# Idle fillers on the tensor engine: fewer, as small products on zeros

## The chip, the cores and the metric

The kernel runs on one core of one Trainium2 chip. The core has five engines with instruction streams of their own: the tensor engine (PE; its loads of the stationary operand are shown as PEld), VectorE (DVE), ScalarE (ACT), GpSimd (POOL) and SyncE (SP), which issues most transfers. The metric is the device time of one execution in microseconds (us), lower is better; the median of several executions is given.

## What is computed

Two stages follow each other. The first is a linear attention with decay, over 4 batches of 8 heads, 768 positions and a head size of 64, computed in blocks. The second multiplies its output, seen as 3072 rows of 512, by `w_in` (512 x 2048), applies a leaky ReLU, and multiplies by `w_out` (2048 x 512). The weights arrive as 64-bit floats and the rest as 32-bit floats.

```python
for b in range(nb):                       # blocks along the sequence
    intra = einsum('bhic,bhjc->bhij', qb, kb) * Dmask
    intra = einsum('bhij,bhjd->bhid', intra, vb)
    inter = einsum('bhid,bhde->bhie', qb * lam_pow, kv_state)
    out[:, :, sl] = intra + inter
    kv_state = lam_block * kv_state + einsum('bhsd,bhse->bhde', kb * rev_pow, vb)
x = out.transpose(0, 2, 1, 3).reshape(B * S, H * D)
h = x @ w_in
g = maximum(0.01 * h, h)
return g @ w_out
```

## The kernel before

The 3072 rows are cut into 24 chunks of 128 positions (index `c`), and four chunks make a group of 512 rows. For each chunk PE transposes k and q (L331), multiplies scores and key-value products in 64 x 64 quadrants into the PSUM tile `psc` and the outputs into `po` (both through `quad`, L286). VectorE multiplies the scores by the decay factors (L375) and adds the state (L380, L382). GpSimd scales k (L345), scaled q (L349) and the state (L385). ScalarE copies the transposes out of PSUM (L340, L341). A tiny copy out of `po` (L414) separates two groups of products that write the same bank.

The output of a chunk is split into three parts `xh`, `xl`, `xm` (L430, L431, L433)[...]. `w_in` is loaded as 64-bit words into three buffers `raw` (L485, issued from ScalarE's queue), put together as 32-bit floats (L497 to L504) and split into `wh`, `wl`, `wm` (L510 to L521). The first layer multiplies these parts (L561), one group of 512 rows and 256 of the 2048 columns at a time; its result goes to DRAM. The second layer reads it back and multiplies by the parts of `w_out` (L620). Loads of k and q (L311, two transfers each) and v (L316) are issued from SP.

The order in which each engine gets its instructions is made by the class `Plan` (L37). Every piece of work is registered with `add`, with an estimated duration and the names of what it reads and writes; `emit` (L81) simulates the engines and sorts the pieces. A second pass in `emit` (from L144) goes through the sorted list with delays that are a little more optimistic, and issues the real instructions. In this pass, the variable `soon` holds when each engine is expected to be free. Where PE is expected to stand idle between `soon["PE"]` and the next piece's time `t`, `plan.idle` is called, which is the function `busy` (L250). It issues transposes of the identity matrix into the bank `b1[0]`, a bank that isn't in use yet: the fillers. Their time isn't added to `soon`. The fillers end for good with the first piece that writes that bank (`plan.spare`, "b10"), a product of the first layer.

Before the planned work, `busy(WARM)` issues 9 fillers (L255). The identity that they read is written by GpSimd, by `make_identity` (L248). `plan.warm` (L258) is where the second pass takes PE to be free for the first time. The tile `raw[-1]` is the third of the buffers for `w_in`; its first load is the third of these loads.

## Time and profile before

| what | before |
|---|---|
| median of 3 runs | 626.7 us (626.27 to 627.1) |
| profiled execution, time | 626.15 us |
| profiled execution, span from first to last instruction | 623.6 us |
| PE busy | 613.9 us, 98% |
| VectorE / ScalarE / GpSimd busy | 297.9 / 281.2 / 91.7 us |
| DMA, mean over the span | 163 GB/s, 101.51 MB |
| fillers (L253) | 38, from 1.36 to 29.66 us |
| first product of the first layer (L561) | 29.46 us |

The page of the profile cuts the span into 40 slices of 15.6 us. PE busy is counted from instructions whose ends are modelled, and weight loads lie beside products on a line of their own. The chain that ended last follows from the last instruction back to what released each step. In a timeline, a line gives the start, the duration, the engine, the line of the code and the operation of a run of like instructions; in square brackets stands how long the engine idled before it and what ended that.

The 38 fillers are the 9 at the start and 29 in eleven idle stretches that the plan expected. In order these hold 2 (at 5.05 us), 6 (6.33), 1 (9.80), 1 (14.40), 1 (15.47), 1 (16.21), 4 (20.64), 2 (22.02), 3 (25.20), 1 (27.94) and 7 (28.68) fillers.

### The profile page before, as it was taken

The page shows a single profiled execution, that of the slowest core. Times are in us where ns is not written, and L with a number is a line of the kernel's source. Part 1 is how long each engine was busy: PE and PEld are TensorE (multiplying, and loading weights), DVE is VectorE, ACT ScalarE, POOL GpSimd, SP SyncE. Part 2 cuts the span into 40 slices and gives each one's busy share as a digit, 9 for nine tenths or more (in the row PEclk, how much of TensorE's full clock was granted, in tenths as well). Part 3 has the DMA queues.
Part 4 walks back from the last instruction along what each step waited for, and adds up shares of the span by engine and source line. Part 5 has one row for each costly group of instructions (what it writes and reads, how often), then busy time and mean ns, then how long its engine had stood idle before and what let it go on. Part 6 is the DMA issues. An engine that isn't in the chain of part 4 may idle for free.

```text
span 623.6 us, 13157 instructions
## 1 busy us (share of the span) xinstructions
PE 613.9 (98%) x5578; PEld 513.5 (82%) x5578; DVE 297.9 (48%) x366; ACT 281.2 (45%) x461; POOL 91.7 (15%) x95
## 2 busy tenths in 40 slices
PE   8899999999999999999999999999999999999997
PEld 7688888898888888888788888888888888888885
DVE  4799882400344333333145763735545454535531
ACT  3688875443577766664444722312222222314111
POOL 4852513300332222222000000000000000000000
PEclk9999999999999999999999999999999999999999
DMA  9998844632787778842455762432524333333201
GB/s 201 250 259 259 243 156 136 155 111 91 206 248 253 245 238 259 247 163 87 169 202 189 247 203 72 153 117 82 188 67 135 136 106 131 128 109 118 85 0 67
DMA packets 103706, 101.51 MB, mean 163 GB/s; under 512 B 78560, under 2 KB 80608, under 8 KB 103648
## 3 DMA queue, kind: packets, MB, share of 16 engines
q1 hardware_dynamic: 99152, 92.29, 47.3%
q10 hardware_dynamic: 4496, 8.39, 4.3%
q8 instruction: 43, 0.70, 0.5%
q14 instruction: 15, 0.12, 0.1%
HBM read 65.02 MB, written 35.65 MB: 161 GB/s over the span
## 4 chain that ended last, share of the span: by engine, by line
PE 96%; DMA 2%; SPq 0%; POOL 0%; DVE 0%; ACT 0%; issue 0%; DVEq 0%
PE b L561 43%; PE b L620 17%; PE po L620 11%; PE psc L620 10%; PE po L286 4%; PE pt L620 3%; PE psc L286 3%; PE po L331 2%; PE pt L331 2%; DMA att<-in_q_dram 2%; PE b L253 1%; DMA att<-in_k_dram 1%; SPq L311 0%; PE b L331 0%; POOL att L345 0%
## 5 line engine op out<-in xcount | busy, mean ns | idle before, releaser
L602 ACT ACTIVATE xh<-att 128x1024 fp32r<-128x1024 f32 x48 | 50.9, 1061 | 147.3 <-PE po L620 141.3
L603 DVE SCALAR_TENSOR_TENSOR xl<-att,xh 128x1024 fp32r<-128x1024 f32 x48 | 58.7, 1223 | 99.4 <-ACT xh L602 99.4
L561 PE MATMUL b<-xh,wh 128*128 128x512 f32 (+3 forms) x416 | 105.5, 377 | 0.0
L561 PE MATMUL b<-xl,wl 128*128 128x512 f32 (+3 forms) x416 | 105.4, 376 | 0.0
L561 PE MATMUL b<-xm,wm 128*128 128x512 f32 (+3 forms) x416 | 104.9, 381 | 0.0
L561 PEld LDWEIGHTS b<-xl,wl 128*128 128x128 f32 x416 | 75.5, 188 | 14.7 <-DVE wl L515 0.2
L561 PEld LDWEIGHTS b<-xh,wh 128*128 128x128 f32 x416 | 75.3, 188 | 14.3
L561 PEld LDWEIGHTS b<-xm,wm 128*128 128x128 f32 x416 | 73.5, 188 | 13.2
L579 ACT ACTIVATE b<-b 128x512 f32<-128x512 f32 (+2 forms) x98 | 56.7, 579 | 57.1 <-PE b L561 56.3
L582 ACT ACTIVATE gs<-b 128x512 f32<-128x512 f32 (+2 forms) x98 | 57.8, 590 | 48.7 <-PE b L561 40.2
L375 DVE TENSOR_TENSOR att<-psc,att 128x512 f32<-128x512 f32 x24 | 16.5, 688 | 128.3 <-PE psc L286 128.2
L620 PE MATMUL b<-wl,xl 128*128 128x512 f32 x192 | 74.7, 389 | 0.0
L620 PE MATMUL b<-wh,xh 128*128 128x512 f32 x192 | 74.7, 389 | 0.0
L605 DVE SCALAR_TENSOR_TENSOR xm<-xl,xh 128x1024 fp32r<-128x1024 f32 x48 | 58.8, 1226 | 4.8
L345 POOL TENSOR_TENSOR att<-att 128x512 f32<-128x512 f32 (+1 forms) x24 | 27.6, 1149 | 141.1 <-PE po L331 133.5
L620 PEld LDWEIGHTS b<-wh,xh 128*128 128x128 f32 x192 | 36.1, 188 | 7.5
L620 PEld LDWEIGHTS b<-wl,xl 128*128 128x128 f32 x192 | 36.0, 188 | 7.5
L385 POOL TENSOR_TENSOR att<-att 128x256 f32<-128x256 f32 x40 | 35.6, 889 | 28.7 <-DVE att L382 23.4
L620 PE MATMUL po<-wm,xm 128*128 128x512 f32 (+1 forms) x100 | 37.2, 381 | 0.7 <-ACT raw L642 0.7
L620 PE MATMUL psc<-wh,xh 128*128 128x512 f32 x96 | 37.4, 389 | 0.0
L620 PE MATMUL po<-wl,xl 128*128 128x512 f32 x96 | 37.4, 389 | 0.0
L620 PE MATMUL b<-wm,xm 128*128 128x512 f32 x96 | 37.4, 389 | 0.0
(67 smaller groups left out, 817.1 us busy)
## 6 DMA issues: line engine op xcount, KB each, us to landing
att<-g SPq DMA_DIRECT2D x48, 512.0 KB, 3.2
g<-gs SPq DMA_DIRECT2D x45, 512.0 KB, 2.9
raw<-in_moe_w_in_dram ACTq DMA_DIRECT2D x16, 512.0 KB, 5.0
raw<-in_moe_w_out_dram SPq DMA_DIRECT2D x16, 512.0 KB, 4.3
att<-in_k_dram SPq DMA_DIRECT2D x48, 128.0 KB, 4.0
att<-in_q_dram SPq DMA_DIRECT2D x48, 128.0 KB, 3.7
att<-in_v_dram SPq DMA_DIRECT2D x24, 256.0 KB, 3.9
out_dram<-gs SPq DMA_DIRECT2D x23, 256.0 KB, 2.2
```

The lines of the kernel that those rows point to most:

```text
L286: nc.tensor.matmul(dst[HALF[cols]], lhsT=lhsT[HALF[rows]], rhs=rhs[HALF[rows]], start=start, stop=True, skip_group_check=True)
L331: nc.tensor.transpose(out=at[y], in_=src[:, 2 * y:2 * y + 2, :].rearrange("p a d -> p (a d)"), identity=ident)
L345: lambda e="POOL": ENG[e].tensor_tensor(kr[nr], kr[nr], _bc(pow_k, 3, D)[nr], op=ALU.mult), ["fk"], [f"k{i}"])
L375: add("DVE", 0.69, lambda: nc.vector.tensor_tensor(sc, psc[:, :, lower, :], decay, op=ALU.mult), ["psc", "fk"], ["sc"])
L385: add("POOL", 0.7, lambda new=new, j=j: nc.gpsimd.tensor_tensor(state[(j + 1) % 4], new, _bc(lam_c, 2, D), op=ALU.mult), [f"st{j % 4}", "f ...
L561: nc.tensor.matmul(dst, lhsT=w[z][:, kk * 2 * P + f * P:kk * 2 * P + (f + 1) * P], rhs=x[z][:, kk, toks], start=start and kk == 0, stop=kk ...
L579: add("ACT", ns, lambda b=b: nc.scalar.activation(out=b, in_=b, func=AF.Copy, bias=0.0, scale=S + 1.0), [], [kb], rank=-1.5)
L582: add("ACT", ns, lambda b=b, r=r: nc.scalar.activation(out=r, in_=b, func=AF.Prelu, bias=0.0, scale=1.0 / WS, alpha=0.01), [kb], [f"gs{jg} ...
L602: add("ACT", 1.05, lambda: nc.scalar.activation(out=h, in_=graw[j], func=AF.Copy, bias=0.0, scale=NEAR), reads, wr("h"))
L603: add("DVE", 1.25, lambda: nc.vector.scalar_tensor_tensor(l, graw[j], 1.0, h.bitcast(F32), op0=ALU.mult, op1=ALU.subtract), reads + [f"rh{ ...
L605: add("DVE", 1.25, lambda: nc.vector.scalar_tensor_tensor(m, l.bitcast(F32), -S, h.bitcast(F32), op0=ALU.mult, op1=ALU.add), [f"rh{j}", f" ...
L620: nc.tensor.matmul(acc[tb][z // 2][:, cols], lhsT=ring[j][z][:, f * T + tb * P:f * T + (tb + 1) * P], rhs=W[pp][z][:, f * d_model:(f + 1) ...
```

## The change

Four things change. The second pass calls for fillers only where the expected idle time is over 1.0 us, not 0.4; and it asks for as many as fit into it less 0.8 us, not less 0.2, at 0.22 us each as before. A filler becomes a product of a 128 x 128 stationary operand with 64 columns, in place of a transpose of 128 columns. The number at the start goes from 9 to 12, and these read a 128 x 128 piece of `raw[-1]` that VectorE fills with zeros, not the identity from GpSimd; the later ones still read the identity. Last, `plan.warm` starts from 0.6 us instead of 1.3: with 12 for 9 fillers it goes from 3.28 to 3.24.

```diff
@@ -150,8 +150,8 @@
             if e == "PE":
                 if self.spare in self.ops[i][4]:
                     self.idle = None
-                if self.idle is not None and t > soon[e] + 0.4:
-                    self.idle(int((t - soon[e] - 0.2) / 0.22))
+                if self.idle is not None and t > soon[e] + 1.0:
+                    self.idle(int((t - soon[e] - 0.8) / 0.22))
             soon[e] = t + ways[e]
@@ -182,7 +182,7 @@
-    WARM = 9
+    WARM = 12
@@ -247,15 +247,17 @@
     nc.scalar.dma_start(out=lam_b, in_=lam.partition_broadcast(P))
     make_identity(nc, ident)
 
-    def busy(n):
+    def busy(n, x=ident):
 
         for _ in range(n):
-            nc.tensor.transpose(out=b1[0][:, 0:P], in_=ident, identity=ident)
-
-    busy(WARM)
+            nc.tensor.matmul(b1[0][:, 0:C2], lhsT=x, rhs=x[:, 0:C2], start=True, stop=True, skip_group_check=True)
+
+    idle = raw[-1][:, 0:P]
+    nc.vector.memset(idle, 0.0)
+    busy(WARM, idle)
     nc.gpsimd.memset(zero, 0.0)
     plan = Plan()
-    plan.idle, plan.spare, plan.warm = busy, "b10", 1.3 + 0.22 * WARM
+    plan.idle, plan.spare, plan.warm = busy, "b10", 0.6 + 0.22 * WARM
```

## The prediction

> **What bounds the kernel now.** I read the page first, then PE's waits, then the chain that ended last over the first 31 us, then the timeline there. From the page:

> ```profile
> PE   8899999999999999999999999999999999999997
> PEclk9999999999999999999999999999999999999999
> DMA  9998844632787778842455762432524333333201
> ```

> Each digit is 15.6 us. PE is full from the third slice on; only slices 0 and 1 leave room, and there DMA is the full one. All waits of PE in the run:

> ```profile
> PE pt L331 <- DMA att<-in_q_dram: 1.5, 2, 0.8
> PE b L253 <- POOL att L256: 1.4, 1, 1.4
> PE psc L286 <- DVE att L382: 1.0, 2, 0.7
> PE po L620 <- ACT raw L642: 0.7, 1, 0.7
> PE po L286 <- ACT att L414: 0.6, 2, 0.3
> PE b L331 <- DMA att<-in_k_dram: 0.5, 1, 0.5
> ```

> That is 5.7 us, and apart from 0.7 at 619 us and 0.3 at 307 us all of it lies before the first product of the first layer (L561). From there PE runs without a break, so only an earlier or later start of L561, at 29.66 us in the chain, can reach the end. The chain up to it (start, length, what):

> ```profile
> 4.01 1.25 PE b L331 x4
> 5.26 0.43 PE b L253 x2
> 5.69 0.85 PE pt L331 x4
> 6.54 1.28 PE b L253 x6
> 7.82 1.55 PE psc L286 x64
> ...
> 12.19 1.21 PE psc L286 x64
> ...
> 15.38 4.93 DMA att<-in_q_dram
> ...
> 20.80 0.44 PE b L253 x4
> 21.24 0.82 PE po L286 x45
> 22.05 4.61 DMA att<-in_q_dram
> ...
> 28.75 0.91 PE b L253 x7
> ```

> The fillers (L253) stand on the chain five times: before q0's transposes, before the first scores, at 20.80, at 28.01 (0.26, not shown) and for 0.91 us right before L561. The two loads of q, 4.93 and 4.61 us from issue to landing against a median of 3.7, lie between.

> [...]four transposes take 0.85 us at 5.69 and 0.44 later, so 0.213 and 0.11 each. [...]between 1.36 and 7.8 PE did nothing but transposes, fillers among them, at half clock; the first products start at 7.75, and within their 1.55 us the distance of four concurrent ones goes from 0.107 to 0.058, at 8.8 us. PEclk doesn't show this change. [...]Here q5's second half, issued at 22.05, lands at 26.66, beside a load of w_in issued from ACT at 22.17.

> **The change part by part.** The sum is made against the profiled execution, 626.15 us with a span of 623.6; the median of three is 626.7, so 0.55 is added at the end.

> *Which fillers are left.* The planned gaps don't change, since fillers don't enter the plan's times. Before, a gap got int((gap-0.2)/0.22) fillers; after, int((gap-0.8)/0.22), and none up to 1.0. From the counts of the timeline (2, 6, 1, 1, 1, 1, 4, 2, 3, 1, 7: 29): the gap of 6 was 1.52 to 1.74 us and gets 3 or 4; that of 4 was 1.08 to 1.30 and gets 1 or 2; that of 3 gets 0 or 1; that of 7 was 1.74 to 1.96 and gets 4 or 5; all others none. So 8 to 12 are left of 29.

> *What one costs.* It loads 128 columns of weights and moves 64, where a transpose moves 128. Weight loads that nothing holds up:

> ```profile
> 4.01 0.29 PEld L331 LDWEIGHTS b<-att 128*128 128x128 f32 x2 [0.87 <-DMA att<-in_k_dram]
> 22.02 0.20 PEld L253 LDWEIGHTS b<-att 128*128 128x128 f32 x2
> ```

> One load alone is 0.18 (slow clock) or 0.14; the second adds 0.11 or 0.06. The 64 columns take 0.107 or 0.058, as the scores show. So a filler takes 0.11 (slow) or 0.06 (full) where load and product overlap, and 0.21 or 0.12 where they don't. I take the lower, since here loads of different products do overlap, and keep both. So a filler covers half of what the transpose did at most, and the plan's 0.22 twice too much.

> *The warm-up.* VectorE's fill is off the trace; its nearest row is GpSimd's fill of the same size, 0.20 us from 0.73. VectorE has nothing to do until 3.43, so nothing queues behind it. PE starts at about 1.0 instead of 1.36, and 12 fillers end between 2.3 (12 x 0.11) and 3.5 (12 x 0.21). The first half of k lands at 3.96 either way: cost nothing, gain nothing. Only the clock could gain. The loads into the third buffer of raw (whose zeros the fillers read) come third in order, at 22.17: no wait there.

> *The first scores.* Without the two fillers at 5.26, q0's transposes are held by q0's landing (5.07 and 5.64) and by their own 0.85: they end at 6.12 instead of 6.54. Then 3 or 4 fillers, 0.33 to 0.84, end by 6.96. Keys and values for psc are there at 6.60 (GpSimd's L345, 5.54 + 1.06) and 6.87 (v's landing). So psc starts at about 6.95 instead of 7.82: PE is 0.85 earlier, 0.3 more if the clock rises earlier. k1's second half lands at 8.05, so its transposes can follow at once, and psc of chunk 1 comes at about 11.3 instead of 12.19.

> *What becomes of that lead.* Behind psc stand the loads of k3 and q3 on SP. But the DMA engines are full: landings follow each other about 0.57 us apart from 4 to 12 us, and the view by windows of one us has their share at 0.96 to 1.37 from 7 to 16 us (packets of several queues are summed) and 0.81 in the next. SP's issues themselves take 1.5 us there instead of 0.5. An earlier issue only fills what was free: 0.2 of the us at 16. q3 then lands between 0 and 0.6 us earlier; I take 0.2, the free time, and 0.6 for the range.

> *The gaps at 20.8 and later.* The four fillers at 20.80 hold po 0.44 us; with one or two short ones po comes 0.3 earlier. That gains nothing: what follows waits for ACT's copy (L414, 22.58), behind three other ACT operations that start with q3's transposes, and then for DVE's L382, until 24.11. The two at 22.02, three at 25.20 and one at 27.94 end before their next operation is released anyway (ACT 22.80, q5 26.71, ACT 28.29).

> *The last gap.* L561 needs xh of chunk 3:

> ```profile
> 28.81 0.60 ACT L430 ACTIVATE xh<-po 128x512 fp32r<-128x512 f32 x1
> ```

> It is there at 29.41; the seven fillers end at 29.66. Four or five short ones end at 28.75 + 0.6 = 29.35 at most. L561 starts at about 29.46: 0.20 gained, the one sure gain. Next late is ACT's xh.

> *After it.* PE is full, but three weight loads of wl (46.88, 56.32, 77.22) waited for DVE's L515 by 0.23, 0.08 and 0.07: DVE's splitting of w_in has no slack there. Part of that work follows PE, since ACT waits for PE's products before it (at 41.27, for one); part hangs on w_in's loads. Either 0.2 + 0.2 = 0.4 us comes through whole, or the wl at 46.88 holds PE and next to nothing does. I take 0.4, because ACT's waits say that the work ahead of this wl moves with PE, and keep 0 for the range.

> Sum: 626.15 - 0.4 = 625.75; with 0.55, 626.3. Range of this case: no gain but the measurement's own spread (626.9) to 0.2 + 0.6 + 0.4 for an earlier clock (625.5).

> **Rivals.**
> *Faster, a reordering of loads.* w_in's second load (issued from ACT at 14.61, landed at 19.2) went ahead of q3 (issued from SP from 13.80 to 15.9, landed at 20.32). If q3's issue moves up by 0.85 and that load, which follows k2's transposes, doesn't, q3 goes first. 768 KB took from 17.17 to 20.32, so 512 KB are 2.1 us; the gain ends where PE is free after k3's transposes, at 19.0: 1.3 to 1.4 us, with the 0.2 at the end 1.6. Against: SP's issue was itself held, and w_in's first load also moves up, since it follows k1's transposes, and takes the room. Time 625.1.
> *Slower, the clock.* Fewer and shorter fillers leave more idle time before L561. [...]PE idles there 0.74 of 4.2 us before (82% busy), and without the fillers 0.3 + 0.75 + 0.35 + 0.4, so 57% busy. For it: that drop. [...]
> *Nothing at all.* Should wl and q5's landing hold everything, 626.7; this lies in the first case's range.

> **How the numbers follow.** What a measurement of this kernel can tell from no change is about 0.2%, 1.25 us. A small gain or nothing: 0.56, nearly all within. Reordering or a stronger effect of the clock: 0.29. The clock lost: 0.15. So faster 0.30, same 0.55, slower 0.15. The range takes in the faster case with half a microsecond more, and stops short of the lost clock: 624.6 to 627.9. The likeliest case's own is 625.5 to 626.9.

> **What would show it.** Right: the first filler near 1.0 and a distance of 0.11 between fillers; 8 to 12 later ones; psc first at about 6.95; q3's transposes not before 20.0; L561 at 29.2 to 29.5; no new wait of PE after it. Wrong: q3's transposes near 19; L561 before 28.5; its eight first products taking more than 3 us (the clock); fillers of 0.2 at full clock; or a first wl that lets PE wait longer than 0.3.

## The result, and the profile after

The changed kernel takes 629.94 us (median of 10) against 626.51 us: a ratio of 1.0052, with a 95% interval of 1.0035 to 1.0068. It is slower, and outside the range that was given. Its profiled execution took 628.63 us, with a span of 626.8 us against 623.6.

In the slices of the page PEclk, the share of PE's full clock that was granted (in tenths), has one digit that is new:

```profile
PEclk9899999999999999999999999999999999999999
```

The 8 is slice 1 (15.6 to 31.3 us): PE's clock was taken down there for a while. Three lines of PE's timeline before, to compare with (start, duration, engine, line, operation, count; idle time before in brackets):

```profile
7.75 1.62 PE L286 MATMUL psc<-att 64*64 64x64 f32 x64
9.31 0.66 PE L331 MATMUL b<-att 128*128 128x128 f32 x4
...
29.46 2.12 PE L561 MATMUL b<-xh,wh 128*128 128x512 f32 x8
```

The timeline of PE in the first 39 us of the changed kernel:

```profile
1.05 5.38 PE L253 MATMUL b<-raw 128*128 128x64 f32 x24 [1.05 <-DVE raw L256]
6.23 1.06 PE L333 MATMUL b<-att 128*128 128x128 f32 x4
...
7.94 1.81 PE L253 MATMUL b<-att 128*128 128x64 f32 x8
9.67 1.99 PE L288 MATMUL psc<-att 64*64 64x64 f32 x64
11.59 1.11 PE L333 MATMUL b<-att 128*128 128x128 f32 x4
...
13.92 0.66 PE L333 MATMUL pt<-att 128*128 128x128 f32 x4
...
20.14 1.77 PE L288 MATMUL psc<-att 64*64 64x64 f32 x64 [1.39 <-DVE att L384]
...
30.69 1.10 PE L253 MATMUL b<-att 128*128 128x64 f32 x8
32.03 2.12 PE L563 MATMUL b<-xh,wh 128*128 128x512 f32 x8 [0.24 <-ACT xh L432]
...
38.83 2.08 PE L563 MATMUL b<-xm,wm 128*128 128x512 f32 x8 [0.85 <-DVE xm L435]
```

(The lines behind the fillers moved by two: L331 is now L333, L286 L288, L561 L563. L253 is the filler in both.) Three things are to be seen.

First, the count. The start has 12 products in the code and 24 instructions here; the gap ahead of the first scores has 4 and shows 8. Each of these 32-bit products shows as two passes, each with its own weight load (24 loads beside the 24 products of the start). At the slow clock a pass takes 5.38 / 24 = 0.22 us (they start 0.213 apart), so a filler takes about 0.43 us; at the full clock, at 30.69, (1.10 - 0.28) / 7 = 0.12 a pass (one pass alone lasts 0.28) and 0.23 a filler. The start block ends at 6.4 us. k's first transpose, 4.01 before, waits until 6.23.

Second, the slow clock lasts. The four transposes at 11.59 still take 1.11 us, and those at 13.92 take 0.66. The trace holds records of the granted clock, which no view prints; the first one, of full clock, begins at 8.81 us before and at 13.62 now.

Third, PE idles 1.39 us before 20.14, and the scores after it take 1.77 in place of 1.16. PE idled because VectorE's sum of the state came late; that the scores then took longer is the clock, as the windows of the changed kernel show; PEclk is the column after the engines' busy times:

```profile
20.00:21.00 1.00, 0.86 (x40) 0.87 (x44) 1.00 (x2) 0.15 (x1) 1.00 (x2) 0.72 1.01 288
21.00:22.00 1.00, 1.00 (x37) 0.88 (x30) 1.00 (x3) 0.00 (x0) 0.88 (x1) 0.50 1.11 261
22.00:23.00 1.00, 1.00 (x6) 1.00 (x7) 1.00 (x4) 0.00 (x0) 0.00 (x0) 0.50 0.97 211
23.00:24.00 1.00, 1.00 (x7) 1.00 (x6) 0.57 (x1) 0.69 (x2) 0.97 (x1) 0.57 0.93 200
```

From 20.4 to 23.9 us PE ran at half clock. This view does show such a fall. It doesn't show the slow clock at the start, since it takes the time ahead of the first record as full clock: it gives 1.00 for 11 to 12 us, where the four transposes take 1.11. The longest waits of PE in the changed kernel, besides the 1.1 us at its start and 0.7 us near its end, as before (in total, times, longest):

```profile
PE psc L288 <- DVE att L384: 1.7, 2, 1.4
PE po L288 <- ACT att L416: 1.2, 3, 0.7
PE b L563 <- DVE xm L435: 0.9, 1, 0.9
```

The waits for q and for k, 2.0 us before, are not among them: PE now comes later than its loads. In their place it waits longer for what other engines make from its own late products.

The first layer begins at 32.03, 2.57 us later than before; that is most of the span's 3.2 us. The last product ends 591.1 us after the first layer's first, against 590.4 before. The new wait of 0.85 at 38.83, where VectorE's `xm` is late, may be the reason for these 0.7 us, which isn't shown: in the profiled executions below this stretch takes from 590.1 to 592.2 us.

### The profile page after: what moved, and what is told of

Read it like the earlier page. It is cut to its first block, busy times and chain, and to the rows that moved or that the text cites. A ratio compares the mean times of both kernels' runs of the same rounds, so it can differ in the third digit from the quotient of the medians.

```text
span 626.8 us, 13172 instructions
## 1 busy us (share of the span) xinstructions
PE 616.9 (98%) x5584; PEld 518.8 (83%) x5584; DVE 298.2 (48%) x367; ACT 281.2 (45%) x461; POOL 92.2 (15%) x95
## 4 chain that ended last, share of the span: by engine, by line
PE 96%; POOL 2%; DVE 1%; issue 0%; ACT 0%; DVEq 0%
PE b L563 42%; PE b L622 17%; PE po L622 10%; PE psc L622 10%; PE po L288 4%; PE psc L288 4%; PE pt L622 3%; PE po L333 2%; PE pt L333 2%; PE b L253 1%; POOL att L387 1%; DVE xm L435 1%; PE b L333 0%; POOL att L347 0%; POOL att L351 0%; DVE w L505 0%
## 5 line engine op out<-in xcount | busy, mean ns | idle before, releaser
L563 PE MATMUL b<-xh,wh 128*128 128x512 f32 (+3 forms) x416 | 105.5, 376 | 0.2 <-ACT xh L432 0.2
L563 PE MATMUL b<-xm,wm 128*128 128x512 f32 (+3 forms) x416 | 104.8, 381 | 0.9 <-DVE xm L435 0.9
L563 PE MATMUL b<-xl,wl 128*128 128x512 f32 (+3 forms) x416 | 105.3, 376 | 0.0
L563 PEld LDWEIGHTS b<-xl,wl 128*128 128x128 f32 x416 | 75.5, 188 | 14.7 <-DVE wl L517 0.2
L563 PEld LDWEIGHTS b<-xh,wh 128*128 128x128 f32 x416 | 75.2, 188 | 14.6 <-ACT xh L432 0.4
L563 PEld LDWEIGHTS b<-xm,wm 128*128 128x128 f32 x416 | 73.5, 188 | 14.1 <-ACT att L342 1.0
L347 POOL TENSOR_TENSOR att<-att 128x512 f32<-128x512 f32 (+1 forms) x24 | 27.9, 1164 | 144.5 <-PE po L333 133.6
L622 PE MATMUL pt<-wm,xm 128*128 128x512 f32 x96 | 37.3, 389 | 0.0
```

The lines of the kernel that those rows point to most:

```text
L347: lambda e="POOL": ENG[e].tensor_tensor(kr[nr], kr[nr], _bc(pow_k, 3, D)[nr], op=ALU.mult), ["fk"], [f"k{i}"])
L563: nc.tensor.matmul(dst, lhsT=w[z][:, kk * 2 * P + f * P:kk * 2 * P + (f + 1) * P], rhs=x[z][:, kk, toks], start=start and kk == 0, stop=kk ...
L622: nc.tensor.matmul(acc[tb][z // 2][:, cols], lhsT=ring[j][z][:, f * T + tb * P:f * T + (tb + 1) * P], rhs=W[pp][z][:, f * d_model:(f + 1) ...
```

## The experiments

Theory L: the fillers' length did it. Theory C: the clock fell because fewer fillers were left. Later a theory K joined: the kind of filler decides when the clock rises.

The table gives each kernel's median and its ratio to the kernel before with the 95% interval. The ratio isn't the quotient of the two medians: for e4 the medians give 1.0014, the means 1.0026, and the ratio is 1.0024. The kernel before was run along in three series of 60, 43 and 35; the second ran on another chip than the first and the third.

"Clock lost" counts the executions whose mean granted clock reads 0.996 or less. One stretch of 3.4 us at half clock costs 0.5 x 3.4 / 624 = 0.0027 of the mean. The profiled executions also have a fall after PE's last product (at 623.2 us before and at 624.6 in the changed kernel). This product ends 3.7 us before the span does, so that fall alone costs at most 0.003. A reading of 0.996 therefore has a fall within the work. One of 0.997 can be either: the profiled execution of e7 reads 0.997 and has one. The number in brackets counts 0.997 too, so the true count lies between the two. The last column is the median of the executions above 0.996. Where the text says when the clock was full in a profiled execution, this is the beginning of the first record.

| kernel | median us | ratio, interval | clock lost (0.997 too) | median of the others |
|---|---|---|---|---|
| before, series 1 (e1 to e4) | 626.27 | | 6 (13) of 60 | 626.20 |
| before, series 2 (e5 to e8) | 626.11 | | 7 (15) of 43 | 626.02 |
| before, series 3 (e9 to e11) | 626.27 | | 6 (8) of 35 | 626.14 |
| the change | 629.94 | 1.0052, 1.0035 to 1.0068 | 9 (9) of 10 | 628.44 (one) |
| e1: the change with 5 products at the start | 626.96 | 1.0019, 1.0008 to 1.0030 | 6 (6) of 22 | 626.88 |
| e2: thresholds alone | 626.39 | 1.0001, 0.9989 to 1.0013 | 8 (10) of 14 | 625.77 |
| e3: start alone | 628.04 | 1.0028, 1.0018 to 1.0037 | 0 (1) of 15 | 628.04 |
| e4: thresholds and late products | 627.16 | 1.0024, 1.0011 to 1.0037 | 10 (10) of 22 | 626.99 |
| e5: 23 transposes at the start | 626.97 | 1.0006, 0.9995 to 1.0017 | 1 (3) of 13 | 626.96 |
| e6: e4 with two transposes for a product | 627.03 | 1.0009, 0.9999 to 1.0020 | 5 (8) of 14 | 626.47 |
| e7: 12 transposes at the start | 626.71 | 1.0009, 0.9995 to 1.0022 | 7 (11) of 14 | 626.17 |
| e8: no filler at the start | 626.72 | 1.0001, 0.9993 to 1.0009 | 5 (5) of 13 | 626.32 |
| e9: e3 with 128 columns | 626.63 | 1.0003, 0.9992 to 1.0014 | 0 (1) of 14 | 626.62 |
| e10: fewer transposes in long gaps only | 625.94 | 0.9991, 0.9980 to 1.0002 | 1 (1) of 14 | 625.84 |
| e11: the change with a filler priced right | 626.49 | 1.0001, 0.9986 to 1.0016 | 7 (9) of 14 | 625.91 |

**e1, the change with a shorter start.**

```diff
-    WARM = 12
+    WARM = 5
-    plan.idle, plan.spare, plan.warm = busy, "b10", 0.6 + 0.22 * WARM
+    plan.idle, plan.spare, plan.warm = busy, "b10", 0.6 + 0.22 * 12
```

> The changed kernel with 5 in place of 12 products ahead of the planned work, and the plan told the same 3.24 us. Theory L (the twelve products, 24 passes of 0.22 us, end at 6.4 us and push everything by 2.2 us): 10 passes end near 3.3 us, k's first transpose is back at 4.0, the first layer starts near 29.3, time 626.0 to 627.0. Rival C (fewer fillers let the clock fall, whatever the start does): the start of the first layer stays near 31 to 32 and the time at 628.5 to 631.

The block ended at 3.45 us and k's first transpose was at 4.09. The ratio fell from 1.0052 to 1.0019, so most of the loss went with the seven products. It did not all go: the first layer began at 30.94, since the four products ahead of the scores took 1.81 us and the clock was full only at 11.5 (four transposes took 1.11 at 9.86 and 0.66 at 12.00). L is right on the larger part; a second cause remains.

**e2, the thresholds alone.**

```diff
-                if self.idle is not None and t > soon[e] + 0.4:
-                    self.idle(int((t - soon[e] - 0.2) / 0.22))
+                if self.idle is not None and t > soon[e] + 1.0:
+                    self.idle(int((t - soon[e] - 0.8) / 0.22))
```

> The kernel before with the two thresholds of the change alone (idle time over 1.0 us, room less 0.8), all fillers transposes. Theory L: no block at the start is longer, so 626.0 to 626.8. Rival C: fewer fillers, the clock falls once in the first 30 us, 628 to 631.

The time is that of before, as L said, but two effects seem to meet in it. The first scores came at 7.29 in place of 7.75 and the first layer at 29.36 in place of 29.46; where the clock held, the median was 625.77, which is 0.43 us under before. But 8 to 10 of 14 executions lost the clock, where before 6 to 13 of 60 did. The profiled one lost it at 28.55, just ahead of the first layer, as PE's timeline of e2 shows:

```profile
28.57 1.12 PE L253 MATMUL b<-att 128*128 128x128 f32 x4
29.36 3.30 PE L561 MATMUL b<-xh,wh 128*128 128x512 f32 x8
```

Four transposes take 1.12 in place of 0.66, and the first eight products 3.30 in place of 2.12. So C is right that fewer fillers cost the clock, and wrong on the size: nothing is left of it in the median.

**e3, the start alone.** The kernel before, with `WARM = 12`, the zeros from VectorE, products for the start only, and `plan.warm` as in the change.

```diff
-    busy(WARM)
+    idle = raw[-1][:, 0:P]
+    nc.vector.memset(idle, 0.0)
+    for _ in range(WARM):
+        nc.tensor.matmul(b1[0][:, 0:C2], lhsT=idle, rhs=idle[:, 0:C2], start=True, stop=True, skip_group_check=True)
```

> The kernel before with the start of the change alone: 12 products on zeros from VectorE; thresholds and later fillers as before. Theory L: k's first transpose at 6.2 us, time 628.5 to 630.5, as the whole change. Rival C: the later fillers keep the clock, so 626 to 627.5.

L's signs came as told: k at 6.23 us, the first layer at 31.22; the time, 628.04, is 0.5 under the band that L gave. None or one of 15 executions lost the clock. The start alone costs 1.8 us.

**e4, everything but the start.** The thresholds of e2, the late fillers as products on the identity, and 9 transposes at the start.

> The kernel before with everything of the change but the start: the thresholds, and later fillers as products on the identity; 9 transposes at the start. Theory L: 626.0 to 627.0. Rival C: 628 to 631.

The median is 0.9 us above that of before, between the two bands. The ratio of 1.0024 and e3's 1.0028 give the 1.0052 of the whole change, so by the ratios the two parts add up; the medians' 0.9 and 1.8 us fall short of its 3.4. Thresholds alone (e2) cost nothing, so the late loss points to the products, though the intervals of e2 and e4 just overlap. PE's timeline of e4, and then that of e3:

```profile
6.28 1.81 PE L253 MATMUL b<-att 128*128 128x64 f32 x8
8.02 1.99 PE L287 MATMUL psc<-att 64*64 64x64 f32 x64
9.94 1.11 PE L332 MATMUL b<-att 128*128 128x128 f32 x4
```

```profile
9.78 1.55 PE L289 MATMUL psc<-att 64*64 64x64 f32 x64
11.26 0.65 PE L334 MATMUL b<-att 128*128 128x128 f32 x4
```

In e4 four products hold the scores back to 8.02, and the clock is still slow at 9.94; it was full at 11.5 (the next four transposes, at 12.04, took 0.65). In e3, after 5.4 us of products on zeros, it was slow too (1.06 at 6.23), and rose at 10.7, during the scores. That led to theory K, that what fills PE's time matters for the clock.

**e5, the start as long, of transposes.**

```diff
-    WARM = 9
+    WARM = 23
-    plan.idle, plan.spare, plan.warm = busy, "b10", 1.3 + 0.22 * WARM
+    plan.idle, plan.spare, plan.warm = busy, "b10", 1.3 + 0.22 * 9
```

> The kernel before with 23 transposes on the identity at the start in place of 9, nothing else: as long as the 12 products (1.36 + 23 x 0.213 = 6.26 us), of the other kind. Theory L (only the length counts): k's first transpose at 6.25, and the time of the start alone again, 627.6 to 628.4. Theory K (the kind counts too: PE busy with transposes raises the clock, short products on zeros don't): the clock is full by 4.8 to 8.2 us, before the first scores, and a part of the loss comes back, 626.8 to 627.5.

PE's timeline of e5:

```profile
1.36 5.17 PE L253 MATMUL b<-att 128*128 128x128 f32 x23 [1.36 <-POOL att L256]
6.32 0.73 PE L331 MATMUL b<-att 128*128 128x128 f32 x4
...
8.29 1.16 PE L286 MATMUL psc<-att 64*64 64x64 f32 x64
```

k's transposes begin at 6.32 and take 0.73 in place of 1.06: the clock is full (at 6.6), and nothing but transposes has run. K's band holds (626.97). The interval, 0.9995 to 1.0017, lies just under that of e3, 1.0018 to 1.0037. So here the clock rose with transposes alone. The same length of the other kind costs about 0.9 us less, by the medians against their own series; the 0.9 us that are left can't be told from nothing by the ratio.

**e9, the same products over 128 columns.**

```diff
-        nc.tensor.matmul(b1[0][:, 0:C2], lhsT=idle, rhs=idle[:, 0:C2], start=True, stop=True, skip_group_check=True)
+        nc.tensor.matmul(b1[0][:, 0:P], lhsT=idle, rhs=idle, start=True, stop=True, skip_group_check=True)
```

> The start of the change alone, with each of the 12 products on zeros over 128 columns in place of 64. A pass of 0.213 us is the weight load's, so the block stays as long and k's first transpose stays at 6.2. Theory D (what raises the clock is the share of time in which columns stream; 64 columns in 0.213 us are too few, 128 as in a transpose are enough): clock full between 4.5 and 8.2 us, time 626.7 to 627.5, as with 23 transposes. Theory Z (zeros don't raise it, whatever the columns): clock full at 10 or later, time 627.6 to 628.4, as with 64 columns.

PE's timeline of e9:

```profile
1.05 4.93 PE L258 MATMUL b<-raw 128*128 128x128 f32 x24 [1.05 <-DVE raw L256]
5.82 0.60 PE L334 MATMUL b<-att 128*128 128x128 f32 x4
...
7.66 1.16 PE L289 MATMUL psc<-att 64*64 64x64 f32 x64
```

The block is even shorter, 4.93 us, because the clock rises within it, at 5.2, and k's transposes take 0.60. The time is 626.63, a little under D's band, and the ratio 1.0003 (0.9992 to 1.0014) lies apart from e3's. It differs from e3 by the number of columns alone, and the operands are zeros in both. So neither the zeros nor the kind of operation made the difference here; twice the columns in the same time did. This is the cleanest pair of the study. (The times of the clock are those of one profiled execution each; the medians are of 15 and 14.)

The pair also tells what the late k costs. SP's issue of the two loads of q3, before, in e3 and in e9:

```profile
13.80 2.09 SPq L311 DMA_DIRECT2D att<-in_q_dram  x2
```

```profile
15.69 2.18 SPq L314 DMA_DIRECT2D att<-in_q_dram  x2
```

```profile
13.24 3.38 SPq L314 DMA_DIRECT2D att<-in_q_dram  x2
```

In e9 k's transposes begin 1.8 us later than before, and still the first scores start at 7.66 (before 7.75) and the loads of q3 are issued no later. In e5, with k at 6.32, the scores start at 8.29 and these loads at 13.80. In e3 the scores start at 9.78 and the loads 1.9 us later than before. So the delay of k alone cost nothing that can be told; with the slow clock behind it, it was carried on.

**e6, the late part with transposes.** As e4, with `range(2 * n)` transposes for n products.

> The late part of the change with each product replaced by two transposes: the same gaps, the same 0.43 or 0.22 us a filler, the other kind. Theory L: first scores near 8.0, first layer near 31, time 626.9 to 627.5, as with products. Theory K: the scores start at the same 8.0, but the clock is full at 7 to 9 us and not at 11.4, and is lost in fewer runs than 10 of 22; time 626.2 to 626.8.

The block ahead of the scores was as long (1.82 us), and the scores came at 8.21 at full clock (1.16 us, against 1.99 in e4): K's sign. The median, 627.03, is in L's band, and 5 to 8 of 14 lost the clock against 10 of 22; the profiled one had it at half from 21.7 to 28.5 us. The intervals of e4 and e6 overlap. How much of the late loss is length and how much the slow clock stays open.

**e7 and e8, more and no fillers at the start.** `WARM = 12` and `WARM = 0` in the kernel before, with `plan.warm` held.

> The kernel before with 12 transposes at the start in place of 9, so that they end at 3.92 us, where k lands, and PE has no break before its own transposes. Theory K: the clock is full [...]between 4.8 and 8.2 us, so the first scores are faster; 625.6 to 626.2, a little under before. Theory L: no difference, 626.0 to 626.6.

> The kernel before without any filler at the start; those in idle times stay. It measures what the start fillers are worth. Theory K: the clock is full no later than 8 to 12 us, since PE is busy from 4.0 on either way; 626.2 to 627.0. Rival (the start fillers pay): the clock comes at 12 or later and the time is 627.0 to 628.5.

With 12 transposes the clock was full at 6.8 us, two us earlier than before (the scores at 7.31 took 1.16), and nothing was gained: 626.71. In its profiled execution PE then ran ahead of the loads and waited 1.2 us for k until 15.55, and the granted clock was 0.5 from 17.0 to 20.4 us; 7 to 11 of 14 executions lost the clock. Without any filler it was full at 10.2, 1.4 us later than before (the scores at 7.81 took 1.99, four transposes at 11.47 took 0.66), and the ratio is 1.0001. So what the start fillers are worth can't be told from nothing here. Outlasting k's landing at 4.0 cost 1.8 us where the clock stayed slow (e3), and nothing that can be told where it rose (e5, e9).

**e10, fewer transposes in long gaps only.**

```diff
-                    self.idle(int((t - soon[e] - 0.2) / 0.22))
+                    self.idle(int((t - soon[e] - (0.2 if t <= soon[e] + 1.0 else 0.8)) / 0.22))
```

> The kernel before; idle times up to 1.0 us get their transposes as before, longer ones get as many as the change gives them (4 for 6 ahead of the first scores, 2 for 4, 4 for 7 ahead of the first layer). If what the thresholds cost is the clock lost in idle times left empty, this keeps most of their gain (0.4 us with the clock held) and loses the clock as seldom as before: 625.6 to 626.0, at best 0.4 under before. Rival: the clock is lost in half of the runs, as with the thresholds alone, 626.2 to 626.8.

625.94, and the clock lost in 1 of 14. e2, which differs only in leaving the short gaps empty, lost it in 8 to 10 of 14: as expected, the fillers in short gaps kept the clock here. The interval, 0.9980 to 1.0002, still holds 1, so a gain of 0.3 us is possible and not shown; in the profiled execution (626.36 us) the first layer began at 30.36, later than before.

**e11, the change with a filler priced right.** `WARM = 5`, and 0.44 for 0.22 in the count.

> The whole change with a filler's price mended: 5 products at the start, and 0.44 us in place of 0.22 each in idle times (2, 1 and 2 products stay). If the loss is the fillers' doubled length and nothing else, all of it is gone: 625.8 to 626.4. If the clock is the second cause, it comes at 11 us again and is lost in over a third of the runs, 626.4 to 627.2.

626.49, ratio 1.0001: the loss is gone. But the clock was full only at 10.8 us (four transposes took 1.11 at 9.11 and 0.66 at 11.30) and was lost in half of the executions or more, in the profiled one (628.48 us) from 17.7 to 21.1 and from 27.9 to 34.7; where it held the median is 625.91. Both hypotheses of the expectation are half right.

## Why the prediction was wrong

*A filler's cost: the step that failed.* I had "0.11 (slow) or 0.06 (full)" for a filler and 0.21 or 0.12 as the upper end. It takes 0.43 and 0.23. A 32-bit product showed as two passes (24 instructions for 12), and a pass with 128 columns of weights lasted 0.213 us at slow clock even with 64 columns moving. The first could be read before: `scores` has 32 products in the code, and the chain showed x64. I read the x64 as products. The second couldn't, since these 32-bit operations with 128 columns of weights were all transposes before; I took the weight load's price from them (0.11 for a second load), where 24 loads of the start's products came 0.213 us apart. With fewer products, the whole change costs nothing that can be told (e11): without the wrong price there is no loss.

*The warm-up* followed from it: an end between 2.3 and 3.5 us, measured 6.4. "Cost nothing" became 1.8 us (e3). A second step failed with it: I took a late rise of the clock to be hidden for the most part behind the loads, an estimate that no trace had shown. The clock rose at 13.6 us in the changed kernel and at 10.7 in e3. With twice the columns it rose at 5.2, and 1.4 of e3's 1.8 us were gone (626.63 against 628.04). So the loss at the start takes both, a block that outlasts k's landing and a clock that stays slow behind it: without the first a rise at 10.2 (e8) or 10.8 (e11) cost nothing that can be told, nor did the block without the second (e9). The start of the warm-up was right (1.05 against about 1.0), as was VectorE's fill (0.17 against 0.20).

*The first scores* were expected at 6.95 us and came at 9.67: the start block ended 2.9 us behind the latest end of the forecast, and four fillers of 0.43 came on top. With transposes (e2) the scores came at 7.29.

*What becomes of a lead* held as far as it went: in e2 the scores were 0.46 us earlier and q3's last transposes started at 20.07 in place of 20.36, where the loads let them. But the opposite doesn't hold. In e3 the scores were 2.0 us late, SP issued q3's loads 1.9 us late, and 1.8 us came through: full queues hid a lead, not a delay.

*The last gap and the sum.* The count of the fillers was right: 10 are left, in 8 to 12. But the 0.20 us of the last gap, "the one sure gain", is a difference between two views: 29.66 is where the chain puts L561, behind the fillers' end, while in the timeline L561 started at 29.46 already, 0.05 us after `xh` was there. Where the clock held, the medians of e2, e10 and e11 lie 0.43, 0.30 and 0.23 us under that of before. That this is near the sum's 0.4 is luck as far as the last gap goes, and with 6 to 13 executions each the gain itself isn't shown.

*The rival of the clock* had a chance of 0.15; its price was an estimate that no trace had shown. Thresholds alone made it happen in 8 of 14 executions, with 1.1 us between their median (626.91) and that of the others; in the whole change it happened in 9 of 10. I held it unlikely on an assumption about the transposes that no trace had shown. In e5 the clock rose at 6.6 us with nothing but transposes run; in e3 it was still slow after 5.4 us of products with half the columns. The rival's own working came close: it had PE 57% busy in 4.2 us ahead of L561, and in e2 the clock fell there after 3.41 us in which PE was busy 55% (1.87 us). In the changed kernel it fell earlier, at 20.4. There the half clock lasted 3.4 us (20.4 to 23.9); in e6 and e11 it also lasted twice that (21.7 to 28.5 and 27.9 to 34.7). In the 3.41 us before each of these falls PE was about half busy (49 to 55%).

*The reordering of loads*: its sign, q3's last transposes near 19 us, was seen in no profiled execution; the earliest were at 20.07 (e2).

## What to carry to other kernels

Read a filler's or any small product's price from the number of instructions in the trace beside the number in the code: a 32-bit product counted double here. Ask of filler work not only when it ends but whether it raises the clock: a block that outlasted k's landing by about 2 us cost 1.8 us with 64 columns moving (e3) and nothing that can be told with 128 (e9). Fillers that end before the landing were worth nothing that can be told (e8). Before thinning fillers out, count the executions that lose the clock, not the median alone: in e2 the median was that of before, and over half of the executions had lost the clock.
